# Odd chunks' attention matmuls moved beside the 64-row matmuls of the first layer, in an mLSTM cell followed by a squared-ReLU feed-forward

## The chip, the cores and the metric

The kernel runs on one core of a Trainium2 chip. A core has TensorE (PE, matrix products; PEld is its weight load), VectorE (DVE), ScalarE (ACT), GpSimd (POOL) and SyncE (SP), which here only issues transfers (SPq). The engines run side by side, each through its own list of instructions in order, and wait for each other by semaphores. The metric is the device time of one execution in microseconds (us).

## The reference

An mLSTM cell over 4 batches x 8 heads x 768 steps with head size 40, and then a feed-forward layer on its output, reshaped to 3072 tokens x 320:

```python
m_new = np.maximum(f_gate[:, :, t] + m, i_gate[:, :, t])
f_stab = np.exp(f_gate[:, :, t] + m - m_new)
i_stab = np.exp(i_gate[:, :, t] - m_new)
C = f_stab * C + i_stab * einsum('bhd,bhe->bhde', vt, kt)
n = f_stab * n + i_stab * kt
h_tilde = einsum('bhde,bhe->bhd', C, qt)
y[:, :, t] = o * h_tilde / np.maximum(np.abs(nq), 1.0)      # nq = n . qt
...
h = np.maximum(x @ w_in, 0.0)          # 320 -> 2048
return (h * h @ w_out)                 # 2048 -> 320
```

## The kernel before

**Tiles.** The 3072 tokens are cut into 24 chunks of 128 steps (chunk s; six to a batch). Inside a chunk the recurrence is computed as attention: scores of all pairs of steps, weighted with decays, times the values, plus the contribution of the state C carried over. Two chunks 2g and 2g+1 make a group g of 256 tokens for the feed-forward layer, twelve groups in all. Its first layer is called F1 here, its second F2; both use a Strassen-like scheme with seven products in place of eight, so sums of their operands are formed on VectorE and GpSimd.

**Stages.** From chunk 6 on, the main loop (`for n, (which, g, i) in enumerate(parts)`, L1031) takes four parts to a stage, `at` = 0 to 3; stage s works on chunk s. From stage 9 on, an odd stage s = 2g+3 runs F1 of group g, so chunks s-3 and s-2, and an even stage s = 2g+6 runs F2 of group g. The instructions are written in the order in which each engine executes them; nothing reorders them afterwards.

**The attention of chunk s.** `score(s)` (`at` 0) is eight matmuls of 40 rows (L429; the trace shows each fp32 matmul as two passes) into two PSUM banks, weighted in place on VectorE (L444). `attend_turned(s)` (`at` 1) is the product of state and q (L519), of values and weights (L528) and the new state's part (L538); VectorE turns the numerators (L545) and updates C (L551). `store_num` (L557) writes the numerators to DRAM, `load_num` (L562, four transfers, waiting for the store) brings them back with steps on the partitions. `normalise_turned` (L574 to L583, `at` 2) divides by the denominator and applies the output gate; `store_rows` (L609) and `load_rows` (L614, four transfers) pass x through DRAM, and `turn_squares` (L621, in stage s+1) finishes the transposed x, called xT. `sums_of_x(g)` (L808, L811, GpSimd, `at` 3 of even stage 2g+2) forms five sums of xT, called xs, for F1.

**F1.** A half of F1 (two to a stage) is `ffn1_open` (four blocks of full 128-row matmuls, L816, into banks X, Y, V, Z) and `ffn1_close` (three more full blocks, then 16 matmuls of 64 rows, L848, for the last 64 of the 320 inputs; ScalarE and VectorE then empty the banks, L852 to L856). Of the four opening blocks the first (X) reads only xT of the even chunk, the second (Y) reads the sum xs[3].

**SyncE's queue.** All transfers of the loop go through it in the order written: per stage store_num, loads of k and v for chunk s+4 (L304), the output gates (L332), load_num, `pair_up(s+3)` (L295, four), store_rows, `load_squares(s+2)` (L317, four), load_rows, `load_A(s+2)` (L342), and the outputs (L778, L783). `load_A` brings in the log decays, which `decays` (L377, ScalarE), `mask` (L367, GpSimd) and `weigh` (L391, ScalarE) turn into weights in the stage ahead of their use. `turn_kq` (L324) and `scale_q` (L492) prepare k and q.

Of the kernel before, what the change touches and what calls it, by code (L numbers as in the profile page):

```python
# [29 lines left out]
def kernel(  # L30
# [31 lines left out]
    NT = B * NB  # L62
# [211 lines left out]
    st = {}  # L274
# [14 lines left out]
    KQ_SQ, X_SQ = 7, 6  # L289
# [36 lines left out]
    def load_o(s):  # L326
        b, c = divmod(s, NB)
        r, (s0, s1) = next((r, (a, z)) for r, (a, z) in enumerate(RUNS) if a <= s < z)
        if s == s0:
            st["og", r] = ld.tile([P, 4, H, D], F32, name="og")  # L330
        og = st.setdefault(s, {})["og"] = st["og", r][:, s - s0]
        nc.sync.dma_start(og, o_gate[b, :, c * P : (c + 1) * P, :].rearrange("h p d -> p h d"))  # L332

    def sigmoid(s):
        nc.scalar.activation(st[s]["og"], st[s]["og"], AF.Sigmoid)
# [86 lines left out]
    def scores(s, o=(False, False)):  # L422
        d = st[s]

        sc = [bank(o[i]) for i in range(2)]
        for j in range(PR):
            for i in range(2):
                rows = slice(DP * i, DP * i + D)
                nc.tensor.matmul(  # L429
                    sc[i][:, j, :], lhsT=d["kT"][rows, j, :], rhs=d["qT"][rows, j, :], start=True, stop=True,  # L430
                )
        d["sc"] = sc

    def weighted(s):
        d = st[s]
        d["P"] = []
        for i in range(2):
            heads = slice(i, H, 2) if s < KQ_SQ else slice(PR * i, PR * (i + 1))
            t = d["W"][:, heads, :]
            if s < W_IN:  # L440
                at = 2 * H * P + W * (2 * (s % 2) + i)
                t = flat_c[:, at : at + W].rearrange("p (j t) -> p j t", j=PR)
            d["P"].append(t)
            nc.vector.tensor_tensor(t, d["sc"][i], d["W"][:, heads, :], op=ALU.mult)  # L444
# [189 lines left out]
    def new_g2(g):  # L634
        if g < 2:
            st["g2", g] = ffn.tile([P, NF, WG], F32, name=f"g2_{g}", bufs=1)
        else:
            st["g2", g] = g2c if g == 2 else st["g2", g - 3]
# [32 lines left out]
    def relu_half():  # L671
        if "half" in st:
            hs, g4 = st.pop("half")
            for i, h in enumerate(hs):
                nc.scalar.activation(g4[:, :, i, :], h[:], AF.Relu)
            st.setdefault("relu", []).append(g4)
# [110 lines left out]
    F11, F12 = win4[0][:, :, 0, :], win4[1][:, :, 0, :]  # L787
    F21, F22 = win4[0][:, :, 1, :], win4[1][:, :, 1, :]
    WS = {}
# [24 lines left out]
    def blocks(to, lhsT, rhs, q, start):  # L814
        for n in range(4):
            nc.tensor.matmul(  # L816
                to[:, n, :], lhsT=lhsT[:, 4 * q + n, :], rhs=rhs, start=(start and n == 0), stop=True,
                skip_group_check=True,
            )

    def ffn1_open(g, q):
        if q == 0:
            new_g2(g)
        xT, xs = st["xT", g], st["xs"]
        X, Y, V, Z = st["f1"] = [ps_h.tile([P, 4, P], F32, name="h_ps") for _ in range(4)]
        m1, U2, U4 = [ffn.tile([P, 4, P], F32, name="r_sb", bufs=4) for _ in range(3)]
        st["U"] = U2, U4
        blocks(X, F11, xT[:, 0, 0, :], q, True)
        nc.scalar.copy(m1[:], X[:])  # L829
        blocks(Y, WS[1], xs[:, 3, :], q, True)  # L830
        nc.vector.tensor_tensor(U2[:], Y[:], m1[:], op=ALU.add)
        blocks(V, WS[0], xs[:, 0, :], q, True)
        nc.vector.tensor_tensor(U4[:], V[:], U2[:], op=ALU.add)
        blocks(Z, F22, xs[:, 4, :], q, True)

    def ffn1_close(g, q):
        xT, xs = st["xT", g], st["xs"]
        (X, Y, V, Z), (U2, U4) = st["f1"], st["U"]
        g4 = st["g2", g][:, 8 * q : 8 * q + 8, :].rearrange("p (n two) t -> p n two t", two=2)
        t0, t1 = slice(0, P), slice(P, 2 * P)  # L840
        blocks(X, F12, xT[:, 0, 1, :], q, False)
        blocks(Y, F21, xs[:, 2, :], q, True)
        blocks(V, WS[3], xT[:, 1, 1, :], q, True)
        lo, hi = slice(0, KR), slice(KR, 2 * KR)
        for pair in (((X, lo, xT[lo, 0, 2, :]), (Y, hi, xT[hi, 1, 2, :])), ((V, lo, xT[lo, 1, 2, :]), (Z, hi, xs[hi, 1, :]))):
            for n in range(4):
                for to, rows, rhs in pair:
                    nc.tensor.matmul(  # L848
                        to[:, n, :], lhsT=w_in2[rows, 4 * q + n, :], rhs=rhs, start=False, stop=True, skip_group_check=True,
                    )  # L850
        tt = nc.vector.tensor_tensor
        nc.scalar.activation(g4[:, :, 0, t0], X[:], AF.Relu)  # L852
        tt(U2[:], U2[:], Y[:], op=ALU.add)  # L853
        tt(g4[:, :, 1, t1], U4[:], Y[:], op=ALU.add)
        tt(g4[:, :, 0, t1], U4[:], V[:], op=ALU.add)
        tt(g4[:, :, 1, t0], U2[:], Z[:], op=ALU.subtract)  # L856
        st["open"] = g4
# [10 lines left out]
    def do(f, s):  # L868
        if 0 <= s < NT:
            f(s)  # L870

    def score(s):
        scores(s)
        weighted(s)
# [84 lines left out]
    for u in range(8):  # L959
        s = 2 + u // 2  # L960
# [67 lines left out]
            parts += [(1, g + 2, i) for i in range(4)]  # L1028
    LAST = (16, 17, 18, 18, 18)
    assert LAST[-1] == len(pieces)  # L1030
    for n, (which, g, i) in enumerate(parts):  # L1031
        s, at = 6 + n // 4, n % 4
        if n == 5:
            brought.close()
            late = ctx.enter_context(tc.tile_pool(name="late", bufs=1, side="right"))
        if at == 0:
            do(score, s)
        if at == 1:
            do(attend_turned, s)
            do(decays, s + 1)  # L1040
            do(mask, s + 1)
            if n > 4:
                do(turn_kq, s + 1)
            do(decay_C, s + 1)
            if s > X_SQ:
                do(turn_squares, s - 1)
            do(store_num, s)
            do(load, s + 4)
            if 8 <= s < 20:
                load_o(s + 4)  # L1050
            do(load_num, s)
            do(pair_up, s + 3)
        if 5 <= n < 8:
            sums_of_weights(n - 5)
        if n == 6:
            sums(1, slice(0, NPAIR), (1, 2))
        if n == 8:
            sums_of_weights(3)
            sums(1, slice(0, NPAIR), (3,))
        if n == 9:  # L1060
            sums(1, slice(0, NPAIR), (4,))
        if which == 2 and 0 < g < NG - 1 and i == 3:
            sums(g + 1, slice(0, NPAIR), (2,))
        if which == 2 and g > 1 and i < 2:
            sums(g, slice(0, NPAIR), (3 + i,))
        if n in (10, 11):
            for more in range(2):
                sums_of_win(2 * (n - 10) + more)
        if at == 3 and s >= 8 and s % 2 == 0 and s // 2 - 1 < NG:
            sums_of_x(s // 2 - 1)  # L1070
        fast = which == 1 and g > 2
        if at == 2 and not fast:
            if n > 4:
                do(scale_q, s + 1)
        if at == 3:
            if s % 4 == 3:
                for r in range(s + 1, min(s + 5, NT)):
                    sigmoid(r)
        if fast:
            (ffn1_close if i % 2 else ffn1_open)(g, i // 2)  # L1080
            if at == 2:
                do(scale_q, s + 1)
        elif which == 1:
            ffn1_main(g, i)
            if i % 2 == 0:
                held = st["half"]
            else:

                both = held, st["half"]
                for more, half in enumerate(both):  # L1090
                    ffn1_rest(g, i - 1 + more, half[0])
                for half in both:
                    st["half"] = half
                    relu_half()
                    square_half()
        elif g == 0:
            ffn2(g, *divmod(i, 2))
        else:
            ffn2_fast(g, i)
        if at == 2:  # L1100
            do(lambda s: weigh(s, masked=True), s + 1)
            ffn1_square()
            if n < 4:
                do(turn_kq, s + 1)
                do(scale_q, s + 1)
            do(normalise_turned, s)
            do(store_rows, s)
            do(load_squares, s + 2)
            do(load_rows, s)
            do(load_A, s + 2)  # L1110
        if at == 0:
            ffn1_square()
        if n < 5:
            while rounding.done < LAST[n]:
                rounding.step()
# [30 lines left out]
```

## Time and profile before

| | us |
|---|---|
| median of 3 runs | 515.89 (513.97 to 516.12) |
| profiled execution, own time | 512.99 |
| its span in the trace | 511.2 |
| TensorE busy | 502.6 (98%) |
| VectorE busy | 347.0 (68%) |
| ScalarE busy | 248.7 (49%) |
| GpSimd busy | 112.7 (22%) |
| an odd stage with F1 (stage 13, 233.3 to 253.4) | 20.1 |
| an even stage with F2 (stage 14, 253.4 to 271.8) | 18.4 |

Times inside the trace count from the start of the span. Matmul ends are modelled by the profiler, so a busy TensorE may still lose time between matmuls of different forms; that is read from the distances of their starts. In the chain of work, each piece is given with its start, its length and the engine, tile and line; "x32" counts passes. The transfers' rows give the time of the issue on the queue, not of the landing.

### The profile page before, as it was taken

The numbers are of one execution on the slowest core, as the hardware profiler recorded it, in microseconds if no ns is written. First come the engines' busy times: TensorE is split into PE (matmuls) and PEld (weight loads), VectorE is DVE, ScalarE is ACT, GpSimd is POOL, SyncE is SP. The second block draws the span as 40 slices with busy tenths as digits, with TensorE's granted clock in tenths as the row PEclk, the third lists the DMA queues.
The fourth block names the chain that finished last, engine by engine and source line by source line (L and its number), as shares of the span: only waits on it lengthen the run. The fifth ranks groups of instructions, "written<-read, shape, count | busy, mean of one in ns | idle before, by whom it ended". The sixth has DMA issues, their size and how long they took to land.

```text
span 511.2 us, 11842 instructions
## 1 busy us (share of the span) xinstructions
PE 502.6 (98%) x4648; PEld 460.9 (90%) x4649; DVE 347.0 (68%) x630; ACT 248.7 (49%) x492; POOL 112.7 (22%) x138
## 2 busy tenths in 40 slices
PE   9999999999999999999999999999999999999997
PEld 4878888787798999999999999999999999999997
DVE  8588966564879767667768777667768666644341
ACT  3768798654440650770660870560861650432400
POOL 3356733312022121112112130122112121020000
PEclk9998999999999999999999999999999999999999
DMA  9999899855675786675675786685655352100000
GB/s 191 207 237 220 246 234 207 135 121 106 115 168 98 167 159 128 153 161 115 158 151 113 172 158 117 161 165 101 165 122 116 94 120 79 46 10 25 0 27 27
DMA packets 238231, 67.63 MB, mean 132 GB/s; under 512 B 185600, under 2 KB 232704, under 8 KB 238176
## 3 DMA queue, kind: packets, MB, share of 16 engines
q1 hardware_dynamic: 238080, 66.68, 61.6%
q8 instruction: 37, 0.61, 0.5%
q10 hardware_dynamic: 96, 0.20, 0.1%
q14 instruction: 18, 0.15, 0.1%
HBM read 54.56 MB, written 17.86 MB: 142 GB/s over the span
## 4 chain that ended last, share of the span: by engine, by line
PE 85%; DVE 8%; ACT 2%; issue 2%; DMA 2%; SPq 1%; POOL 0%; DVEq 0%; POOLq 0%; ACTq 0%
PE h_ps L742 32%; PE h_ps L816 21%; PE h_ps L848 7%; PE h_ps L651 6%; PE tp L429 4%; PE h_ps L688 3%; PE numT L528 3%; PE numT L519 2%; PE h_ps L662 2%; DVE mag L217 2%; PE hp L467 1%; DMA A_bc<-a_rows 1%; PE A_ps L358 1%; PE dC L538 1%; ACT g_c L391 1%
## 5 line engine op out<-in xcount | busy, mean ns | idle before, releaser
L367 POOL TENSOR_SCALAR_AFFINE_SELECT A_bc<-A_bc 128x1024 f32<-128x1024 f32 x22 | 25.5, 1161 | 215.0 <-ACT kq L377 170.0
L742 PE MATMUL h_ps<-T,S 128*128 128x160 f32 x352 | 51.4, 299 | 0.0
L742 PE MATMUL h_ps<-w_out,g 128*128 128x160 f32 x336 | 49.2, 303 | 0.0
L742 PEld LDWEIGHTS h_ps<-T,S 128*128 128x128 f32 x352 | 49.0, 190 | 0.0
L377 ACT ACTIVATE kq<-A_bc 64x512 f32<-64x512 f32 x30 | 18.9, 630 | 61.1 <-DMA A_bc<-a_rows 60.8
L391 ACT ACTIVATE A_bc<-A_bc,b_T 128x128 f32<-128x128 f32 x144 | 44.3, 391 | 8.4 <-POOL A_bc L367 7.9
L742 PEld LDWEIGHTS h_ps<-w_out,g 128*128 128x128 f32 x336 | 46.1, 190 | 1.1
L651 PE MATMUL h_ps<-xT,w_in 128*128 128x256 f32 x192 | 44.5, 386 | 1.6 <-ACT xT L630 1.6
L651 PEld LDWEIGHTS h_ps<-xT,w_in 128*128 128x128 f32 x192 | 36.1, 193 | 7.3 <-ACT xT L630 2.0
L829 ACT COPY r_sb<-h_ps 128x512 f32<-128x512 f32 x18 | 10.5, 586 | 63.8 <-PE h_ps L816 63.8
L816 PE MATMUL h_ps<-xT,w_in 128*128 128x128 f32 x288 | 40.7, 284 | 0.4 <-ACT r_sb L829 0.4
L758 DVE TENSOR_TENSOR y_sb<-y_sb,h_ps 128x160 f32<-128x160 f32 x44 | 14.1, 320 | 36.7 <-PE h_ps L742 36.6
L816 PE MATMUL h_ps<-xs,w_in 128*128 128x128 f32 x288 | 38.0, 275 | 0.0
L816 PEld LDWEIGHTS h_ps<-xT,w_in 128*128 128x128 f32 x288 | 34.9, 191 | 3.4 <-ACT r_sb L829 0.6
L848 PE MATMUL h_ps<-xT,w_in 64*128 64x128 f32 x432 | 36.9, 280 | 0.0
L848 PEld LDWEIGHTS h_ps<-xT,w_in 64*128 64x128 f32 x432 | 33.4, 187 | 2.2
L816 PE MATMUL h_ps<-xs,WS 128*128 128x128 f32 x288 | 35.1, 275 | 0.0
L816 PEld LDWEIGHTS h_ps<-xs,w_in 128*128 128x128 f32 x288 | 35.1, 192 | 0.0
L816 PEld LDWEIGHTS h_ps<-xs,WS 128*128 128x128 f32 x288 | 33.6, 192 | 0.0
L545 DVE STREAM_TRANSPOSE tn<-numT 128x256 f32<-128x256 f32 x36 | 15.9, 449 | 21.2 <-PE numT L528 21.2
L853 DVE TENSOR_TENSOR r_sb<-r_sb,h_ps 128x512 f32<-128x512 f32 x18 | 12.4, 686 | 25.7 <-PE h_ps L848 25.6
L444 DVE TENSOR_TENSOR A_bc<-tp,A_bc 128x512 f32<-128x512 f32 x36 | 23.1, 684 | 9.5 <-PE tp L429 9.5
(168 smaller groups left out, 1069.9 us busy)
## 6 DMA issues: line engine op xcount, KB each, us to landing
A_bc<-a_rows SPq DMA_DIRECT2D x22, 512.0 KB, 4.6
raw<-in_moe_w_out_dram SPq DMA_DIRECT2D x8, 640.0 KB, 4.7
num_rows<-tn SPq DMA_DIRECT2D x18, 256.0 KB, 3.0
kq<-num_rows SPq DMA_DIRECT2D x72, 64.0 KB, 2.6
kqT<-kq_rows SPq DMA_DIRECT2D x34, 128.0 KB, 3.2
raw<-in_moe_w_in_dram SPq DMA_DIRECT2D x8, 512.0 KB, 5.9
kq<-in_k_dram SPq DMA_DIRECT2D x24, 160.0 KB, 4.9
va<-in_v_dram SPq DMA_DIRECT2D x24, 160.0 KB, 5.2
```

What stands on the lines that cost most here:

```text
L367: nc.gpsimd.affine_select(A[:], A[:], compare_op=ALU.is_ge, fill=-1e30, base=0, pattern=[[0, H], [1, P]], channel_multiplier=-1,)
L377: nc.scalar.activation(e[rows], st[s]["A"][0][rows, PR * i : PR * (i + 1), :], AF.Exp)
L391: nc.scalar.activation(d["W"][:, i * n + h, :], A[i][:, h, :], AF.Exp, bias=b_T[:, b, c, i * n + h : i * n + h + 1],)
L429: nc.tensor.matmul(sc[i][:, j, :], lhsT=d["kT"][rows, j, :], rhs=d["qT"][rows, j, :], start=True, stop=True,)
L444: nc.vector.tensor_tensor(t, d["sc"][i], d["W"][:, heads, :], op=ALU.mult)
L528: nc.tensor.matmul(numT[i][halves[g], e, :], lhsT=va_w[s % NKQ][:, h * D1 : h * D1 + DP], rhs=d["P"][h % 2][:, h // 2, :] if s < KQ_SQ els ...
L545: nc.vector.transpose(to[:, 2 * i : 2 * i + 2], numT[i][:, :2, :].rearrange("p c t -> p (c t)"))
L651: nc.tensor.matmul(hs[i][:, n, :], lhsT=w_in[:, a, fb * P : (fb + 1) * P], rhs=xT[:, :, a, :], start=(n == 0 and a == 0), stop=False,)
L688: nc.tensor.matmul(o_ps, lhsT=st["g2", g][:, fb, j * P : (j + 1) * P], rhs=w_out[:, fb, :], start=(fb == 0), stop=(fb == NF - 1),)
L742: nc.tensor.matmul(to, lhsT=lhsT[:, p], rhs=rhs[:, p, :], start=(start and p == 0), stop=(p == NPAIR - 1), skip_group_check=True,)
L816: nc.tensor.matmul(to[:, n, :], lhsT=lhsT[:, 4 * q + n, :], rhs=rhs, start=(start and n == 0), stop=True, skip_group_check=True,)
L848: nc.tensor.matmul(to[:, n, :], lhsT=w_in2[rows, 4 * q + n, :], rhs=rhs, start=False, stop=True, skip_group_check=True,)
```

## The change

It concerns the eight odd chunks 9, 11, ... 23 (`behind(s)`). Their scores are issued behind the 64-row matmuls of the first half of F1, and not at the start of the stage. Their values product stands in the second half, between its full and its 64-row matmuls, for which `ffn1_close` is split in two (`ffn1_rows` is the new second part). What follows the values goes with them: decay_C, store_num, the loads of k and v, load_num, pair_up and load_A stand at the end of the stage. The normalisation of such a chunk and its store_rows and load_rows move into part 1 of the next even stage, behind that stage's own values, store_num, load_num, pair_up and load_o; turn_squares moves from its part 1 to its part 3.

```diff
     def ffn1_close(g, q):
         xT, xs = st["xT", g], st["xs"]
+        X, Y, V, Z = st["f1"]
+        blocks(X, F12, xT[:, 0, 1, :], q, False)
+        blocks(Y, F21, xs[:, 2, :], q, True)
+        blocks(V, WS[3], xT[:, 1, 1, :], q, True)
+
+    def ffn1_rows(g, q):
+        xT, xs = st["xT", g], st["xs"]
         (X, Y, V, Z), (U2, U4) = st["f1"], st["U"]
...
-        blocks(X, F12, xT[:, 0, 1, :], q, False)
-        blocks(Y, F21, xs[:, 2, :], q, True)
-        blocks(V, WS[3], xT[:, 1, 1, :], q, True)
...
+    def after_values(s):
+        do(decay_C, s + 1)
+        do(store_num, s)
+        do(load, s + 4)
+        do(load_num, s)
+        do(pair_up, s + 3)
+
+    def rows_of(s):
+        do(normalise_turned, s)
+        do(store_rows, s)
+        do(load_rows, s)
+
+    def behind(s):
+        return s > 8 and s % 2 == 1 and s < NT
...
-        if at == 0:
+        if at == 0 and not behind(s):
             do(score, s)
         if at == 1:
-            do(attend_turned, s)
+            if not behind(s):
+                do(attend_turned, s)
             do(decays, s + 1)
             do(mask, s + 1)
             if n > 4:
                 do(turn_kq, s + 1)
-            do(decay_C, s + 1)
-            if s > X_SQ:
+            if s > X_SQ and not behind(s - 1):
                 do(turn_squares, s - 1)
-            do(store_num, s)
-            do(load, s + 4)
+            if not behind(s):
+                after_values(s)
             if 8 <= s < 20:
                 load_o(s + 4)
-            do(load_num, s)
-            do(pair_up, s + 3)
+            if behind(s - 1):
+                rows_of(s - 1)
+        if at == 3 and behind(s - 1):
+            do(turn_squares, s - 1)
...
         if fast:
-            (ffn1_close if i % 2 else ffn1_open)(g, i // 2)
-            if at == 2:
+            if i % 2 == 0:
+                ffn1_open(g, i // 2)
+            else:
+                ffn1_close(g, i // 2)
+                if at == 3 and behind(s):
+                    attend_turned(s)
+                ffn1_rows(g, i // 2)
+                if at == 1 and behind(s):
+                    score(s)
+                if at == 3 and behind(s):
+                    after_values(s)
+                    do(load_A, s + 2)
+            if at == (3 if behind(s) else 2):
                 do(scale_q, s + 1)
...
-            do(normalise_turned, s)
-            do(store_rows, s)
-            do(load_squares, s + 2)
-            do(load_rows, s)
-            do(load_A, s + 2)
+            if behind(s):
+                do(load_squares, s + 2)
+            else:
+                do(normalise_turned, s)
+                do(store_rows, s)
+                do(load_squares, s + 2)
+                do(load_rows, s)
+                do(load_A, s + 2)
```

## The prediction

> **What bounds the kernel now.** I read the page's busy shares first, then the chain of work in order of time, then SyncE's queue (SPq) beside it, and last the landing times of the transfers.
>
> The busy shares:
>
> ```profile
> PE 502.6 (98%) x4648; PEld 460.9 (90%) x4649; DVE 347.0 (68%) x630; ACT 248.7 (49%) x492; POOL 112.7 (22%) x138
> ```
>
> TensorE has next to no idle time, so only two things can move the end: TensorE's own work, or a new gap in it. The chain (start us, us, what), one odd stage (13) and the start of the even stage behind it (14):
>
> ```profile
> 233.37 1.09 PE tp L429 x16
> 234.46 3.77 PE h_ps L816 x32
> 238.22 0.60 PE numT L519 x16
> 238.82 1.02 PE numT L528 x16
> 240.15 2.88 PE h_ps L816 x24
> 243.03 1.99 PE h_ps L848 x32
> 245.01 6.45 PE h_ps L816 x56
> 251.46 1.99 PE h_ps L848 x32
> 253.45 0.89 PE tp L429 x16
> 254.34 4.54 PE h_ps L742 x32
> 258.88 0.60 PE numT L519 x16
> 259.48 1.02 PE numT L528 x16
> ```
>
> The same sixteen score passes (L429) take 1.09 us behind full matmuls and 0.89 us behind the 64-row ones (L848). Thirty-two L848 passes take 1.99 us, twice 0.89 is 1.78. So entering the 64-row form costs 0.20 us. The runs of full F1 passes (L816) have 32, 24 and 56 passes in 3.77, 2.88 and 6.45 us: the differences give 0.112 us a pass, and each run carries 0.19 us on top, the way back.
>
> SyncE's queue in stage 14 (start, us, what):
>
> ```profile
> 261.03 0.34 SPq L557 DMA_DIRECT2D num_rows<-tn  x1
> ...
> 262.68 1.43 SPq L332 DMA_DIRECT2D og<-in_o_gate_dram  x1
> 264.20 3.19 SPq L562 DMA_DIRECT2D kq<-num_rows  x4
> 267.44 1.19 SPq L295 DMA_DIRECT2D kq_rows<-in_k_dram  x2
> ...
> 272.61 0.38 SPq L609 DMA_DIRECT2D x_rows<-x_sb  x1
> ```
>
> The queue runs in order. The read-back of the numerators (L562) waits for their store (L557) to land, 3.2 us, and everything written after it waits too. Its four issues and the pairing copies fill the queue to 269.9. Landing times, last column median us, and GpSimd's sums of x at the end of stage 14:
>
> ```profile
> x_rows<-x_sb SPq DMA_DIRECT2D x18, 192.0 KB, 2.1
> xT<-x_rows SPq DMA_DIRECT2D x72, 48.0 KB, 2.4
> ```
>
> ```profile
> 269.59 1.14 POOL L808 TENSOR_TENSOR xs<-xT 128x128 f32<-128x128 f32 x2
> 270.69 0.45 POOL L811 TENSOR_TENSOR xs<-xs,xT 128x128 f32<-128x128 f32 x1
> ```
>
> Those sums of x feed the second block of F1 (Y). Before, they have a whole stage of slack: chunk 13's rows are stored at 252.44 and turned (L621) at 262.75.
>
> **What the Trainium skill says.** "TensorEngine Tiling (Array Packing)", Tiling Modes: "Changing tiling mode (not just tile) drains the TensorE". The trace agrees, at 0.2 us a switch. "DMA: Bandwidth & Descriptors", Anatomy of one DMA: a semaphore wait is done by the issuing sequencer, and a transfer has about 2 us of fixed cost, mostly completion. The trace agrees: SPq's L562 waits for num_rows 15.8 us in total, and 192 KB take 2.1 us. "TensorE: Matmul & The Clock Gate", Part 1: an idle window of about 3.4 us halves the clock, a busy one restores it. Here the clock was 0.50 from 42 to 44 us, after a gap of 1.1 us at 38 us, and eight transposes took 1.74 us there where the same eight take 0.91 us elsewhere (58.8 us).
>
> **The change part by part.** Zero is the start of an even stage's second-layer (F2) work, 254.34 above.
>
> *Scores and values moved on TensorE.* Before, an odd stage enters the 64-row form three times (L429, and L848 twice) and goes back to full passes three times ahead of its L816 runs. After, L816 follows F2 directly, the scores follow L848, and the values (L519, L528, L538) stand between full passes and L848. In the compiled order one entry and two returns go: 3 x 0.2 = 0.6 us. The entry from the values' last form (L538) into L848 is not in this trace. I take it as 0.2, like the others; 0 to 0.4 bounds it. Odd stages 9 to 23 are eight: **-4.8 us** (-6.4 to -3.2).
>
> *Vector and Scalar work moved.* The weighting (L444), the turns of the numerators (L545) and the C updates (L551) move with their matmuls. In even stages VectorE must still scale q (0.7) and weight (1.3) before L528, 5.1 us into F2. Behind the last sums of F1, which end near +1.5, this is done by +3.5: hidden by F2's first two products, and without that cover 2 us a stage. The banks of the next scores are freed by L545, 0.9 us, under 2 us of L848. Scores(s+1) so cost nothing. In stage 9 VectorE is late with sums of weights until 161.4; with no scores and values in between, TensorE reaches block Y's second use at 160.9 while L831 ends at 162.1: +1.2, less the 0.45 us wait for L444 that goes: **+0.8**. The 0.4 us wait for ACT in stage 21 goes: **-0.4**.
>
> *Rows of odd chunks delayed.* Here the cost lies. normalise, store_rows and load_rows of odd chunk s move to the next even stage, **behind** that stage's own store_num, loads, load_num, pair_up and load_o in SyncE's queue; the turn (L621) moves to its last quarter, ahead of sums_of_x. VectorE is not the limit: chunk 13's values end 3 us ahead of F2 (L848 1.99, scores 0.99), so its numerators are stored at -2.7, landed at +0.5 and read back at about +4.3, and normalise runs at about +8.5 to +11 behind L324. The queue is:
> - store_num(14) is issued at 6.7 (261.03), lands at 9.9 (264.20); read-back issued until 13.0; pair_up until 15.6 (269.9);
> - og, now behind these instead of inside the landing wait: 0.6 to 1.4, say 0.9: 16.5;
> - store_rows(13) lands 2.1 later: 18.6; four load_rows at 0.5 each, the last issued at 20.2, landed at 22.6;
> - L621 0.54: 23.2; sums of x to the third, 1.14 + 0.45: 24.8.
>
> TensorE finishes F2 at +17.54 (271.88 above), does block X, which needs only the even chunk, and wants Y's operand at 18.5. Gap: 24.8 - 18.5 = **6.3 us**. VectorE also holds F2's last sum behind L621, which is over before Y ends. Bounds: the quickest stage (12) has pair_up done at 13.6; with og inside that and landings of 1.8, Y's operand comes at 21.1, gap 2.6. load_A(s+2) now stands just ahead of store_num(s+1); where that order occurs before, in stage 21, the store took 6.2 us to land instead of 3.2 (394.73 to 400.96), and og can take 3.0: gap 11.4.
>
> Full queues stand ahead of F1 in stages 11, 13, 15, 17 and 19: 5 x 6.3 = 31.5. Stage 20 has no loads and no og: stage 21 waits 5.3. Stage 22 has no pair_up either, and its read-back ends at 12.2 (417.56 + 2.84, less 408.15): stage 23 waits 2.1. Stage 24 has no chunk, so stage 25 waits for nothing. Sum **+38.9**.
>
> *The later A loads.* load_A of the even chunk is queued behind the late rows, at about +27.5, landing at +32 to +33; ScalarE then runs decays (1.27) and L856, due when the second half's Y opens, near +34.5. TensorE is late itself, so I take 0; without that cover up to 1 us a stage.
>
> *Clock.* Six gaps exceed a window. One half-rate window costs at most 1.7 us of matmuls; a part of it falls in the gap: 1.2 each, **+7** (0 to 16).
>
> Sum: -4.8 + 0.8 - 0.4 + 38.9 + 7 = +41.5 on the profiled execution's own 512.99 us (span 511.2), 554.5. The median, 515.89, is 2.9 above that execution: **557 us**.
>
> **The rivals.**
> - *The saving alone, faster.* If the rows come in time: 515.9 - 4.8 + 0.4 = 511.5. This decides if store_rows is issued by 10.2 (18.5 less the 8.3 us from issue to sums). For it: VectorE could normalise by then, and a transfer needs only 2 us. Against it: store_num's landing alone ends at 9.9, with eight issues still behind it in order. 0.05.
> - *Short gaps.* All landings at their quick end: five of 2.6, then 2 and 0, no lost clock: -4.4 + 15 = +10.6, 526. For it: stage 12. Against: load_A ahead of the store. 0.10.
> - *The store always lands behind load_A.* Gaps of 9 to 11 us: 5 x 10 + 8 + 4, clock 10, less 4.4: +68, 584. For it: stage 21. Against: in stage 14 load_A came 2 us before the store, which still landed in 3.2. 0.08.
> - *Gap and saving cancel (no change).* That needs gaps of 0.6 us a stage, below every case above. 0.02.
>
> **How the numbers follow.** The forecast's own case, gaps of 4 to 8 us, has 0.75. The range 533 to 584 leaves out the first, second and last rivals and half of the third. A measurement of this kernel can tell about 0.5% from no change: faster 0.05, same 0.02, slower 0.93.
>
> **What would show it.** In the changed profile TensorE's busy share falls to some 91%, with seven gaps before an L816 that reads xs, released by POOL L808 or L811, and those by DVE L621, and that by the xT transfer; L609 of odd chunks stands after L332 in the queue, some 16 us into F2. L429 falls near 0.99 us in odd stages, and one 128-row run per half has 56 passes. The granted clock dips behind the gaps. I am wrong if the odd chunks' L621 ends within 16.5 us of the start of F2 (then there is no gap), or, on the saving, if L848 behind L538 takes more than 2.2 us.

## The result: 570.0 us, and the profile after

The changed kernel takes 570.04 us (median of 4 runs, 567.53 to 575.36) where the kernel before, run beside it, takes 515.32: a ratio of 1.1078 (95% interval 1.0996 to 1.1161), slower by 54.7 us. The forecast was 557 us, within 533 to 584. The profiled execution took 567.53 us, its span is 565.7 us, 54.5 more than the 511.2 of before. The ratios here and below count fast runs alone; the one slow run, of rows_early in experiment 8 (546.45 us), is in that kernel's median of 543.39 us (542.37 without it).

The busy shares and the granted clock of the kernel after, from the page:

```profile
PE 510.2 (90%) x4649; PEld 470.1 (83%) x4649; DVE 340.8 (60%) x630; ACT 248.6 (44%) x492; POOL 113.5 (20%) x138
...
PEclk9999999999999979979998997997998899999999
```

TensorE's share falls from 98% to 90%, and from about 200 us on its clock dips six times, in the odd stages 11 to 21. The waits of the kernel after (engine, what it waited for, us in total, times, longest):

```profile
PE h_ps L816 <- POOL xs L811: 45.2, 8, 8.2
DVE xT L621 <- DMA xT<-x_rows: 29.7, 8, 5.8
```

Before, TensorE had no wait for POOL at all. Now one wait, eight times, makes 45.2 us. The chain of work of the kernel after, from stage 13's first half of F1 to the same place of stage 15, and last the same passes in stage 25 (start, length, what):

```profile
250.78 7.46 PE h_ps L816 x48
258.24 1.99 PE h_ps L852 x32
260.22 0.89 PE tp L429 x16
261.12 6.45 PE h_ps L816 x56
...
269.49 1.99 PE h_ps L852 x32
...
272.37 4.54 PE h_ps L742 x32
...
279.06 3.88 DMA num_rows<-tn
283.34 0.93 SPq L562
288.46 2.73 DMA x_rows<-x_sb
292.60 2.21 DMA xT<-x_rows
295.64 1.22 issue
296.86 0.72 POOL xs L808
298.04 7.71 PE h_ps L816 x48
...
516.04 5.62 PE h_ps L816 x48
```

Two things are to be read here. The chain leaves TensorE in F2 and runs over two round trips through DRAM: numerators of chunk 14, then rows of chunk 13. And the 48 full passes behind the gap take 7.46 and 7.71 us. At full clock they take 5.62, as in stage 25. (L852 here is L848 of before.)

SyncE's queue of the kernel after in stage 14, and behind it VectorE, GpSimd and TensorE (the bracket is the idle time just before, and what ended it):

```profile
279.06 0.35 SPq L557 DMA_DIRECT2D num_rows<-tn  x1
...
282.96 2.26 SPq L562 DMA_DIRECT2D kq<-num_rows  x4
285.26 1.20 SPq L295 DMA_DIRECT2D kq_rows<-in_k_dram  x2
...
287.77 0.59 SPq L332 DMA_DIRECT2D og<-in_o_gate_dram  x1
288.46 0.53 SPq L609 DMA_DIRECT2D x_rows<-x_sb  x1
291.21 1.86 SPq L614 DMA_DIRECT2D xT<-x_rows  x4
```

```profile
294.89 0.58 DVE L621 STREAM_TRANSPOSE xT<-xT 128x384 f32<-128x384 f32 x1 [5.09 <-DMA xT<-x_rows]
```

```profile
295.55 2.02 POOL L808 TENSOR_TENSOR xs<-xT 128x128 f32<-128x128 f32 x2 [7.57 <-DVE xT L621]
297.54 0.45 POOL L811 TENSOR_TENSOR xs<-xs,xT 128x128 f32<-128x128 f32 x1
```

```profile
298.04 3.78 PE L816 MATMUL h_ps<-xs,WS 128*128 128x128 f32 x16 [7.24 <-POOL xs L811]
```

F2 starts at 272.30. Counted from there, store_num is issued at 6.8 and store_rows at 16.2 (forecast 16.5). The rows' read-back starts at 18.9 (18.6), L621 is done at 23.2 (23.2), the third sum at 25.7 (24.8). TensorE was idle for 7.24 us before Y.

Where the 54.5 us come from:

| term | forecast | measured |
|---|---|---|
| mode switches saved, eight stages | -4.8 | -4.8 (8 x 0.60, measured in one pair of stages of another kernel, experiment 11) |
| waits in stages 9 and 21 | +0.8, -0.4 | +0.75 (1.20 for L831, less 0.45), -0.4 |
| gaps before Y | +38.9 | +45.2 |
| clock | +7 | +11.5 |
| restarts behind a gap | none | +2.2 |
| sum | +41.5 | +54.5 |

The clock's term is the sum over the six long gaps of what 48 passes took above 5.62 us (7.06, 7.46, 7.71, 7.45, 8.26, 7.31). A restart is the difference between X (0.9 us) plus 48 passes (5.62) and an unbroken run of 56 (6.25): 0.27 us, eight times. The sum meets the 54.5 us of the span more closely than its terms are known: 0.5 us of the span's growth lies ahead of stage 8's F2 (139.11 us against 138.62), where the two kernels do the same.

### The profile page after: what moved, and what is told of

It reads as the page before. It is cut to its first block, busy times and chain, and to the rows that moved or that the text cites. A ratio compares the mean times of both kernels' runs of the same rounds, so it can differ in the third digit from the quotient of the medians.

```text
span 565.7 us, 11849 instructions
## 1 busy us (share of the span) xinstructions
PE 510.2 (90%) x4649; PEld 470.1 (83%) x4649; DVE 340.8 (60%) x630; ACT 248.6 (44%) x492; POOL 113.5 (20%) x138
## 4 chain that ended last, share of the span: by engine, by line
PE 72%; DMA 11%; SPq 6%; DVE 4%; issue 3%; POOL 2%; ACT 1%; POOLq 0%; DVEq 0%
PE h_ps L816 21%; PE h_ps L742 18%; PE h_ps L651 6%; PE h_ps L852 6%; DMA x_rows<-x_sb 4%; PE tp L429 3%; PE h_ps L688 3%; DMA num_rows<-tn 3%; PE numT L528 3%; SPq L614 2%; PE hp L467 2%; PE h_ps L662 2%; PE numT L519 2%; SPq L562 2%; DMA xT<-x_rows 2%
## 5 line engine op out<-in xcount | busy, mean ns | idle before, releaser
L816 PE MATMUL h_ps<-xs,WS 128*128 128x128 f32 x288 | 46.0, 326 | 45.2 <-POOL xs L811 45.2
L816 PEld LDWEIGHTS h_ps<-xs,WS 128*128 128x128 f32 x288 | 43.1, 237 | 46.8 <-POOL xs L811 46.8
L377 ACT ACTIVATE kq<-A_bc 64x512 f32<-64x512 f32 x30 | 18.9, 628 | 77.0 <-DMA A_bc<-a_rows 65.8
L742 PE MATMUL h_ps<-T,S 128*128 128x160 f32 x352 | 51.4, 299 | 0.0
L742 PE MATMUL h_ps<-w_out,g 128*128 128x160 f32 x336 | 49.2, 303 | 0.0
L742 PEld LDWEIGHTS h_ps<-T,S 128*128 128x128 f32 x352 | 49.0, 190 | 0.0
L742 PEld LDWEIGHTS h_ps<-w_out,g 128*128 128x128 f32 x336 | 46.1, 190 | 1.1
L651 PE MATMUL h_ps<-xT,w_in 128*128 128x256 f32 x192 | 44.2, 383 | 2.3 <-ACT xT L630 1.6
L816 PE MATMUL h_ps<-xs,w_in 128*128 128x128 f32 x288 | 39.7, 283 | 1.2 <-DVE r_sb L831 1.2
L816 PE MATMUL h_ps<-xT,w_in 128*128 128x128 f32 x288 | 39.1, 279 | 0.0
L816 PEld LDWEIGHTS h_ps<-xs,w_in 128*128 128x128 f32 x288 | 37.0, 201 | 1.4 <-DVE r_sb L831 1.4
L829 ACT COPY r_sb<-h_ps 128x512 f32<-128x512 f32 x18 | 10.5, 585 | 61.5 <-PE h_ps L816 61.5
L808 POOL TENSOR_TENSOR xs<-xT 128x128 f32<-128x128 f32 (+1 forms) x18 | 18.7, 1058 | 91.7 <-DVE xT L621 80.2
L852 PE MATMUL h_ps<-xT,w_in 64*128 64x128 f32 x432 | 36.9, 280 | 0.0
L816 PEld LDWEIGHTS h_ps<-xT,w_in 128*128 128x128 f32 x288 | 35.4, 193 | 1.1
L852 PEld LDWEIGHTS h_ps<-xT,w_in 64*128 64x128 f32 x432 | 33.4, 187 | 2.0 <-issue 0.5
L857 DVE TENSOR_TENSOR r_sb<-r_sb,h_ps 128x512 f32<-128x512 f32 x18 | 12.3, 686 | 31.0 <-PE h_ps L852 31.0
L831 DVE TENSOR_TENSOR r_sb<-h_ps,r_sb 128x512 f32<-128x512 f32 x18 | 12.4, 690 | 27.3 <-PE h_ps L816 25.6
```

Of the source, the lines that this page charges most:

```text
L377: nc.scalar.activation(e[rows], st[s]["A"][0][rows, PR * i : PR * (i + 1), :], AF.Exp)
L651: nc.tensor.matmul(hs[i][:, n, :], lhsT=w_in[:, a, fb * P : (fb + 1) * P], rhs=xT[:, :, a, :], start=(n == 0 and a == 0), stop=False,)
L742: nc.tensor.matmul(to, lhsT=lhsT[:, p], rhs=rhs[:, p, :], start=(start and p == 0), stop=(p == NPAIR - 1), skip_group_check=True,)
L808: sub = lambda to, a, b: nc.gpsimd.tensor_tensor(to, a, b, op=ALU.subtract)
L816: nc.tensor.matmul(to[:, n, :], lhsT=lhsT[:, 4 * q + n, :], rhs=rhs, start=(start and n == 0), stop=True, skip_group_check=True,)
L852: nc.tensor.matmul(to[:, n, :], lhsT=w_in2[rows, 4 * q + n, :], rhs=rhs, start=False, stop=True, skip_group_check=True,)
```

## The experiments

The theory on record: the loss is the late place of odd chunks' rows in SyncE's in-order queue, and the clock on top of it. Its rivals: the late values themselves, VectorE's order, and load_A. All runs are timed against the kernel before, run beside them. Each diff shows the lines of the loop that matter.

**1. The rows alone (rows_late_only).** The kernel before, with scores, values and everything else of the odd chunks in their old place; only their rows and the turn are late.

```diff
+            if behind(s - 1):
+                rows_of(s - 1)          # behind pair_up(s + 3)
+        if at == 3 and behind(s - 1):
+            do(turn_squares, s - 1)
...
-            do(normalise_turned, s)
-            do(store_rows, s)
-            do(load_squares, s + 2)
-            do(load_rows, s)
-            do(load_A, s + 2)
+            if behind(s):
+                do(load_squares, s + 2)
+                do(load_A, s + 2)
+            else:                       # as before
...
```

> Only the rows of the odd chunks are late (normalise, store_rows, load_rows behind the next even stage's own transfers, the turn in its last quarter); scores and values stand where they stood before. Theory (the order on SyncE's queue makes the gaps): the third sum of x ends about 25.5 us into F2 as in the changed kernel, Y is wanted at 19.6 since the scores still stand ahead of F1: gaps of about 5.9 us in five stages, 4 and 1 in two more, 35 us, with some 11 us of lost clock and 2 us of restarts: about 563 us. Rival (the late values make the rows late): no gaps, 514 to 518 us.

558.12 us, 1.0853 (1.0819 to 1.0887), some 5 us under the 563 expected, with 28.2 us of gaps instead of 35. The same wait appears:

```profile
PE h_ps L816 <- POOL xs L811: 28.2, 8, 5.4
```

So the late rows and their late turn make most of the loss without any late value, and with load_A in its old place. The kernel's span is 44.2 us longer, of which 28.2 are gaps and 16.2 are busy time of TensorE (518.8 against 502.6), at a clock of 0.96. The gap of stage 15 is 4.43 us here and 7.24 after the change. Counted from the start of F2, Y is wanted 1.3 us later here, since the next scores still stand ahead of F1; the rows' store goes out 1.0 us earlier, mostly since og goes out inside a landing wait; and that store lands in 2.23 us instead of 2.73 (0.5). These make the 2.8.

**2. The pairing copies and the gates taken from ahead of the rows (pairs_behind).** The changed kernel, with pair_up and the gates behind the rows in even stages.

```diff
-        do(pair_up, s + 3)
+        if not behind(s - 1):
+            do(pair_up, s + 3)
...
-            if 8 <= s < 20:
+            if 8 <= s < 20 and not behind(s - 1):
                 load_o(s + 4)
             if behind(s - 1):
                 rows_of(s - 1)
+                do(pair_up, s + 3)
+                if s < 20:
+                    load_o(s + 4)
```

> The changed kernel with pair_up and the output gates of the even stages put behind the late rows. Theory: store_rows comes 3.1 us earlier in five stages and 2.5 in a sixth, so the gaps sum to 27 us in place of 45; with gaps of 3 to 5 us a part of the lost clock goes too: 546 to 552 us. Rival (the landing of the transfers under load, not their place in the queue, decides): gaps within 3 us of 45 in sum, 566 to 572 us.

544.97 us, 1.0585 (1.0533 to 1.0636), gaps 24.8 us: a little under the 546 to 552 us and the 27 us expected. Nothing but the order of the queue was changed, and 25 us came back. The gaps of 2.90 and 3.36 us kept the full clock (48 passes in 5.62 us), while the shorter ones of 2.51 and 3.14 us lost it (7.10 and 8.37), like those of 3.8 to 5 us (7.91 to 8.20). The length of a gap alone doesn't decide; the part on the clock below shows what does.

**3 and 4. Work put into the gap (filled_gap, filled_long).** The changed kernel with 22, then 36, extra matmuls of zeros between X and Y in stages 11 to 21. Block Y starts its sum anew in the same bank.

```diff
         nc.scalar.copy(m1[:], X[:])
+        if q == 0 and 4 <= g <= 9:
+            for _ in range(22):          # 36 in filled_long
+                nc.tensor.matmul(
+                    Y[:].rearrange("p n t -> p (n t)"), lhsT=zeros[:, :1].to_broadcast([P, P]),
+                    rhs=zeros[:, :1].to_broadcast([P, W]), start=True, stop=True, skip_group_check=True,
+                )
         blocks(Y, WS[1], xs[:, 3, :], q, True)
```

> The changed kernel with 22 matmuls of zeros (bf16, 128x512, about 0.22 us each, results overwritten) between blocks X and Y of the first F1 half in stages 11 to 21, where TensorE waits. They fill some 4.8 us of gaps of 5.5 to 8.2 us. Theory (the clock gate costs 11.5 us behind the gaps): the 48 passes behind the gap take 5.6 us in place of 7.1 to 8.3, and the time falls by 10 to 12, to about 559 us. Rival (the passes are slow there because of the transfers and sums running beside them, or a mere restart): 48 passes still above 7 us, 568 to 572 us.

> filled_gap with 36 matmuls of zeros in place of 22, some 8.2 us, so that no gap over 2 us is left in stages 11 to 21. Theory (a gap of 2.9 to 4 us was left, which was enough to halve the clock in five stages): the clock stays at 1, the 48 passes take 5.6 us, and the time is 558 to 563 us, since the filling is up to 1.5 us longer than some gaps. Rival (matmuls of zeros in bf16 don't keep the clock up): 48 passes above 7 us, 570 us or more.

With 22 the time was 567.58 us, 1.1034 (1.0995 to 1.1074): a miss. In the filled stages gaps of 1.2 to 4.0 us were left. Four of the six still lost clock (48 passes in 7.25 us, once 7.95); the two with 1.2 and 2.4 us did not (5.62). The rival on record also had passes above 7 us, and 568 to 572 us: taken alone the run decides nothing. With 36 the gaps in these stages are closed but for 1.42 us in stage 19, and there the clock stays up:

```profile
PEclk9989999999999999999999999999999999999999
```

561.86 us, 1.0934 (1.0882 to 1.0987). The 36 take 8.04 us in each of six stages and 3.9 us of gaps remain: 52.1 us of standing or empty work against 45.2, 6.9 more. Yet the kernel is 7.4 us faster than the changed one (the two ratios' difference, 0.0144, of 515). So the clock and the restarts cost about 14 us, give or take 5 by the two intervals; the sum above books 13.7 for them, of which some 2 us are left in filled_long too (a half-rate window in stage 23, three restarts). Behind the zeros, with no gap at all, the 48 passes take 5.36 us (5.54 in stage 15), and behind a short gap 5.62: this is the restart by itself.

**5 and 6. The rows ahead of all else (rows_first, rows_first_turned).** The changed kernel with the rows ahead of store_num. In the second kernel the turn stands ahead of the even chunk's normalisation too.

```diff
+            if behind(s - 1):
+                rows_of(s - 1)          # part 1, ahead of after_values(s)
...
-            if behind(s - 1):
-                rows_of(s - 1)
```

```diff
-        if at == 3 and behind(s - 1):
-            do(turn_squares, s - 1)
...
             else:
+                if behind(s - 1):
+                    do(turn_squares, s - 1)
                 do(normalise_turned, s)
```

> The changed kernel with normalise, store_rows and load_rows of the odd chunk behind the even stage's values but ahead of its store_num on SyncE's queue. Theory: the gaps in front of the blocks that read xs fall from 45 us to under 8 in sum. But everything behind on the queue gets later, load_A of the next even chunk at about 27.5 us after the start of F2; it lands at 32 to 33, decays and L856 end near 34.6, and the second F1 half wants its banks at 27.7: new waits of up to 7 us a stage on ACT, so 530 to 554 us. Rival 1 (the transfers' own length is what is too long): the xs gaps stay above 30 us and the time at 560 or more. Rival 2 (load_A has slack): 511 to 516 us.

> rows_first with L621 of the odd chunk ahead of the even chunk's normalisation on VectorE. Theory: in rows_first the rows had landed near 15.5 us into F2, and L621 waited on VectorE behind L574 until the even chunk's numerators were there (19.3); so the gaps before the blocks that read xs fall from 43.6 us to under 5 in sum. Then load_A, still issued near 27 us into F2, is late for ScalarE, and L856 holds the second F1 half by up to 6 us a stage: 530 to 552 us. Rival (load_A has slack, as rows_first showed no such wait): 509 to 516 us. Second rival (the order on VectorE does not matter): gaps still above 35 us, 565 us or more.

rows_first took 570.47 us, 1.1094 (1.107 to 1.1117), with gaps of 43.6 us in all: no better than the change. My theory of the queue alone fell here. These are the numbers of rival 1, but not for its reason: the rows had landed at about 288.3; VectorE in stage 14 of rows_first shows why that didn't help:

```profile
292.21 0.17 DVE L574 TENSOR_SCALAR dm<-kq 128x8 f32<-128x8 f32 x1 [3.55 <-DMA kq<-num_rows]
...
293.93 0.57 DVE L621 STREAM_TRANSPOSE xT<-xT 128x384 f32<-128x384 f32 x1
```

The turn of chunk 13 stands behind the normalisation of chunk 14 in VectorE's own order. That one waits for numerators that the early rows have now pushed back, so a second in-order queue holds Y. rows_first_turned took 541.22 us, 1.0522 (1.0466 to 1.0577). In stage 14 the turn is done by 281.5, and the wait for POOL is all but gone, but the same late normalisation now holds L831 and, behind late turns, L857 and L858:

```profile
PE h_ps L816 <- DVE r_sb L831: 11.0, 8, 1.8
PE h_ps L816 <- DVE g L858: 5.5, 3, 2.4
PE h_ps L816 <- DVE g_c L858: 4.7, 2, 2.6
...
PE h_ps L816 <- POOL xs L811: 1.0, 3, 0.4
```

The time lies within the 530 to 552 us expected, but by luck: the theory had laid it to the late A loads. These cost TensorE only 0.6 us that shows (L829, which stands on ScalarE behind the decays that wait for them).

**7 and 8. The rows between store and read-back (rows_between, rows_early).** The odd chunk is normalised right behind the even chunk's values; its rows' two transfers stand in the landing waits of the numerators' two, and load_A right behind the read-back. rows_early normalises the odd chunk, and stores its rows, ahead of the even chunk's values.

```diff
     def after_values(s):
         do(decay_C, s + 1)
         do(store_num, s)
+        if behind(s - 1):
+            do(store_rows, s - 1)       # rows_early: ahead of attend_turned(s)
         do(load, s + 4)
+        if behind(s - 1):
+            do(load_rows, s - 1)
         do(load_num, s)
+        if behind(s - 1):
+            do(load_A, s + 2)
         do(pair_up, s + 3)
```

> The changed kernel with the odd chunk's rows threaded through the even stage's transfers: normalise right behind the even chunk's values, store_rows behind store_num, load_rows behind the loads of k and v and ahead of load_num, and load_A behind load_num and ahead of pair_up. Theory: the third sum of x ends 18.7 to 19.5 us into F2 and is wanted at 18.4, so gaps are under 1 us a stage and the clock stays at 1; the mode switches saved then show: 4.8 us less than before, less 0.75 in stage 9 and up to 4 us of small gaps, 511 to 515 us. Rival (late values cost something by themselves on VectorE or ScalarE): above 518 us.

> As rows_between, but normalise and store_rows of the odd chunk stand ahead of the even chunk's values and store_num. Theory: N of the odd chunk lands 4.5 to 5 us into F2, store_rows is issued at about 6.5 and load_rows by 10, so the sums of x are done by 17 and there is no gap at all; store_num of the even chunk is 1 us later at most, which has slack: 510 to 513 us, up to 4 us below rows_between. Rival (normalise delays the turn of the even chunk's numerators and with it everything on the queue): no faster than rows_between.

551.95 us, 1.0733 (1.0698 to 1.0768), gaps 28.5 us; and 543.39 us, 1.0585 (1.0555 to 1.0615), gaps 20.1 us. Both missed, for the reason of rows_first. VectorE of rows_early in stage 14:

```profile
284.17 0.17 DVE L574 TENSOR_SCALAR dm<-kq 128x8 f32<-128x8 f32 x1 [0.48 <-DMA kq<-num_rows]
...
285.95 0.58 DVE L621 STREAM_TRANSPOSE xT<-xT 128x384 f32<-128x384 f32 x1
```

The turn no longer waits for its own data, only for its turn on VectorE.

**9. The turn put first as well (rows_turned).** rows_early with L621 of the odd chunk in part 2, ahead of F2's sums there.

```diff
-        if at == 3 and behind(s - 1):
-            do(turn_squares, s - 1)
...
         if at == 2 and not fast:
             if n > 4:
                 do(scale_q, s + 1)
+            if behind(s - 1):
+                do(turn_squares, s - 1)
```

> rows_early with the turn of the odd chunk's rows (L621) moved on VectorE from behind the even chunk's normalisation to the start of part 2, ahead of F2's third product's sums. Theory (in rows_early L621 stood ready but behind L574, which waited for the even chunk's numerators to land at 16.3 us into F2): L621 ends at 15.3, the third sum of x at 17.9, Y is wanted at 18.4: no gap, no half clock. Then the saved mode switches show, -4.8 us, less the 1.2 us wait in stage 9 and up to 1 us: 509 to 513 us. Rival (the rows cannot come in time in any order): gaps of 2 us or more stay, above 525 us.

519.79 us, 1.0115 (1.007 to 1.0159). Of the waits for POOL 0.2 us are left, and the clock is 1.000: of the 54.7 us, all but some 6 are back, with late values and late rows still in place. The time missed the expectation of 509 to 513; small waits had come up:

```profile
PE h_ps L742 <- DVE y_sb L758: 3.0, 3, 1.8
PE h_ps L816 <- DVE g L858: 2.1, 2, 1.2
...
PE h_ps L816 <- DVE r_sb L831: 1.2, 1, 1.2
```

VectorE waited 2.38 us for xT to land, with F2's addition (L758) queued behind it.

**10 and 11. VectorE's order settled (rows_settled, rows_settled_turns).** First the turn goes behind the first addition of F2's step 2. Then, in odd stages, the turns of k, q and of the even rows go behind the closing sums of F1's first half, and stage 9 is left as before.

```diff
             add(u22, m1, X)
+            late_turn()                 # turn_squares(s - 1) where behind(s - 1)
             if g + 1 < NG:
```

```diff
-        return s > 8 and s % 2 == 1 and s < NT
+        return s > 10 and s % 2 == 1 and s < NT
...
-            if n > 4:
+            if n > 4 and not behind(s):
                 do(turn_kq, s + 1)
-            if s > X_SQ and not behind(s - 1):
+            if s > X_SQ and not behind(s - 1) and not behind(s):
                 do(turn_squares, s - 1)
...
+        if at == 2 and behind(s):
+            do(turn_kq, s + 1)
+            do(turn_squares, s - 1)
```

> rows_turned with one instruction moved: the odd chunk's transposition (L621) stands behind the first addition of F2's step 2 on VectorE, instead of ahead of it. Theory: in rows_turned VectorE waited for xT to land with that addition behind the transposition, so F2's step 3 waited for PSUM three times, 3.0 us in all. Expected: no wait of an L742 for L758, no wait of an L816 for POOL, 516 to 517 us. Rival: the transposition, a microsecond later, brings a wait of the L816 of Y for POOL (the sums of x take 1.6 to 2.5 us), and with it the loss comes back: 518 to 522 us.

> rows_settled, with the turns of k, q and of the even chunk's rows in odd stages put behind the first half's closing sums (L857 to L860) on VectorE, and stage 9 left as in the kernel before. Theory: the waits of rows_turned for g L858 (2.1 us) and r_sb L831 (1.2 us) go, at the cost of one stage's saving (0.6 us): 513 to 515 us, a microsecond or two under rows_settled and about the time of the kernel before. Rival: k^T and q^T come too late for the next scores, an L429 waits for VectorE L324 by a microsecond or more a stage: 517 us and more.

rows_settled: 519.41 us, 1.0105 (1.0064 to 1.0147). The three L742 waits are gone as expected, but the time isn't: 1.8 us of waits for POOL are back, and those for the closing sums (L859 here) went from 2.5 to 4.0 us. The time is in the rival's range (518 to 522), and the rival's wait is there. rows_settled_turns: 511.69 us against 514.26, a ratio of 0.9955 (0.9938 to 0.9973): 0.45% faster than the kernel before, a small gain but with an interval clear of 1, and under the 513 to 515 expected. The waits of TensorE (L817 is L816 of the others):

```profile
PE h_ps L817 <- POOL xs L812: 1.6, 2, 1.1
PE h_ps L651 <- ACT xT L630: 1.6, 2, 1.1
```

The second line is also in the kernel before. No L429 waits, so that rival fell.

This kernel shows the saving, too. Stages 10 and 11 run there without a gap at full clock. The chain of work of the kernel before, from one F2 to the next, and then that of rows_settled_turns, which leaves TensorE in the values:

```profile
178.22 4.54 PE h_ps L742 x32
...
216.43 4.54 PE h_ps L742 x32
```

```profile
182.47 4.54 PE h_ps L742 x32
...
200.00 6.25 PE h_ps L817 x56
206.26 1.99 PE h_ps L853 x32
208.24 0.89 PE tp L429 x16
209.13 6.45 PE h_ps L817 x56
```

Before, the two stages take 216.43 - 178.22 = 38.21 us. In rows_settled_turns the next F2's first matmul starts at 220.01 in the timeline, and that of the line at 182.47 at 182.40 (a chain's piece starts where the one before ends): 37.61 us. The saving is 0.60 us, three switches of 0.20. Seven stages of it are 4.2 us; less the 1.6 us of waits for POOL and a restart behind each of the two, some 2 are left. From stage 8's F2 to the end the profiled execution is 2.2 us shorter than that of before (370.4 against 372.6), and the medians differ by 2.6. The profiled execution as a whole (515.08 us, the slowest of 17) is not shorter: ahead of stage 8's F2, where the kernels do the same, it lost 4.3 us (142.87 against 138.62), in part to 10.24 us at half clock.

## Why the prediction was right, and where it was off

**The saving (-4.8): right.** L852 behind the values' last form takes 1.99 us, as behind full passes, so the entry costs the 0.2 that I took; the scores take 0.89 in odd stages (0.99 was forecast); and the whole is 0.60 in a pair of stages.

**Rows of odd chunks delayed: right in mechanism.** The chain runs over the transfers in the order forecast, L609 stands behind L332 16.2 us into F2, and experiments 1 and 2 show that the rows' place in the queue, and how much stands ahead of it, set the gap. The rival of a saving alone failed where I had put its decision: store_rows went out at 16.2, not by 10.2.

**The gaps (+38.9): too small by 6.3 us.** By stage, from 11 to 25, 6.68, 8.24, 7.24, 8.07, 6.98, 5.54, 2.13 and 0.36 us, where I had five of 6.3, then 5.3, 2.1 and 0. The step that failed is "sums of x to the third, 1.14 + 0.45". In each of the six long gaps the two L808 took 2.02 or 2.03 us, 0.9 more than that: 5.3 of the 6.3 us. Beside them VectorE ran a 128x1024 fp32 addition (L737, in stage 14 from 295.39), where before it ran the short operations of the normalisation. The thirteen traces bear this out: of 117 such pairs the 98 beside an L737 took 1.97 to 3.19 us; of the 19 others 15 took 1.14, also where VectorE was idle, and four beside an L492 took 1.6. No run moved L737 alone. The rest is landings: the rows' store took 2.3 to 4.0 us where 2.1 was taken. (The section on DMA that the prediction cites for about 2 us a transfer is on transfers that GpSimd issues; these are SyncE's.) The landing of the numerators' store, 3.88 us in the chain instead of 3.2, was within the bounds; the queue behind it was quicker in turn. "The store always lands behind load_A" didn't come: no gap reached 9 us.

**VectorE "is not the limit": right for the order of the change, and no further.** There L621 waited 5.09 us for its transfer. With the rows early, VectorE's order kept the gap (experiments 5, 7 and 8). I had let SyncE's queue alone decide on the rival of the saving alone (store_rows by 10.2): it needed VectorE's order as well, and rows_settled_turns, which has both, is the one that got there, with the change in seven of the eight stages.

**The clock (+7): too small, 11.5.** The step "one half-rate window" failed. In the record of the clock every stretch but the last is a whole multiple of 3.41 us, so the clock is set window by window, on a fixed grid. Stage 15 by these windows (start and end; length, busy TensorE and the number of its matmul passes, and so on; the granted clock is the third figure from the right):

```profile
292.19:295.61 3.42, 0.00 (x0) 0.00 (x0) 0.72 (x2) 0.00 (x0) 0.06 (x1) 1.00 0.73 165
295.61:299.02 3.41, 0.98 (x4) 0.98 (x5) 1.20 (x2) 0.00 (x0) 2.83 (x4) 0.50 0.95 108
299.02:302.44 3.42, 3.42 (x18) 3.42 (x17) 1.27 (x2) 0.00 (x0) 0.00 (x0) 0.50 0.69 155
302.44:305.85 3.41, 3.41 (x32) 3.29 (x32) 1.72 (x3) 1.26 (x2) 0.57 (x1) 1.00 0.54 137
```

The gap fills the first window and reaches into the second, and two windows, 6.83 us, have half the clock. So it was behind five of the six long gaps; behind stage 19's it was three, 10.24 us. Of this, 2.4 to 4.7 us fell into the gap, and the rest cost 1.4 to 2.6 us each.

For shorter gaps it is their place on the grid that counts. In pairs_behind the gap of stage 15 (2.90 us) lay across two windows, and that of stage 19 (3.14 us) mostly in one:

```profile
284.60:288.01 3.41, 1.52 (x13) 1.33 (x11) 2.40 (x5) 0.59 (x1) 1.48 (x2) 1.00 0.50 115
288.01:291.43 3.42, 2.41 (x21) 2.41 (x22) 1.01 (x2) 0.00 (x0) 1.41 (x3) 1.00 1.02 201
...
366.53:369.94 3.41, 1.31 (x12) 1.12 (x10) 2.20 (x5) 0.59 (x1) 1.45 (x2) 1.00 0.47 113
369.94:373.35 3.41, 2.37 (x11) 2.37 (x12) 0.18 (x1) 0.00 (x0) 1.45 (x3) 0.50 1.03 203
373.35:376.77 3.42, 3.42 (x18) 3.42 (x18) 1.20 (x2) 0.00 (x0) 0.00 (x0) 0.50 0.57 68
```

With 1.89 and 1.01 us idle in its two windows stage 15 kept the full clock; with 2.10 us in one, stage 19 lost it. From 190 us on, in all thirteen traces: of the windows at full clock, all 35 with more than 2.0 us of idle TensorE were followed by one at half, and none of the 1121 with less than 1.5 us; of the 25 between, eight were. A window at half was followed by another at half where TensorE idled 0.76 us or more in it (29 cases), and by full clock where it idled 0.60 us or less (43).

"TensorE: Matmul & The Clock Gate", Part 1, of the Trainium skill gives an idle window of about 3.4 us as the trigger. The steps of 3.41 us agree with it; the trigger doesn't, since here 2 us of idle time within a window were enough.

**Not foreseen: the restart,** 0.27 us a gap, 2.2 us in all.

**The later A loads (0), stages 9 and 21: right.** No wait of TensorE for the A loads or for L856 appeared, 1.20 us was forecast and measured for L831 in stage 9, and the 0.4 us of stage 21 went.

## What to carry to other kernels

Moving a matmul to save a mode switch moves everything that its result feeds, and each of those steps takes its place in other in-order queues, here SyncE's and then VectorE's. Follow the moved data to its next use on TensorE before counting the saving: here 4.8 us of saving stood against 45 us of gaps, and most of it was to be had only after the rows' transfers, their normalisation and turn, load_A and the turns of k, q and the even rows had been placed anew. A gap of a few microseconds can cost more than its length: price the restart with it, and the clock where 2 us of it fall within one 3.41 us window.

## What the runs showed of the hardware

- The clock went to half behind a 3.41 us window of a fixed grid in which TensorE had idled more than 2.0 us, never behind one with less than 1.5 us (windows from 190 us on, all traces). Gaps of 5.5 us and more always lost it, for 6.83 us or 10.24, and 48 passes took 7.04 to 8.50 us instead of 5.62. With the same gap of 2.13 us in stage 23, the changed kernel kept it (1.24 us in one window, 0.89 in the next; 5.62 us) and filled_long lost it (all in one window; 7.25 us).
- In the start-up a window with 1.09 us idle was enough (before, 37.99 to 41.40 us; the next one had half the clock). What tells it from those of the main loop stays open.
- Matmuls of zeros hold the clock: with 36 of them in the gap it was 0.993 over the span, with the gap open 0.960.
- Shorter gaps can cost more clock than long ones: in rows_late_only, with 28.2 us of gaps, 27.0 us of TensorE's work ran at half the clock (37.6 us at half from stage 11 on, 10.5 of them in gaps); after the change, with 45.2 us of gaps, 24.3 us did (44.4, of which 20.1 in gaps).
- The two GpSimd additions of 128x128 fp32 took 1.97 us and more beside a 128x1024 fp32 addition on VectorE, and 1.14 us beside short operations or none.
